# A new start and a split last tile for a one-core transformer block: c loaded as four rows, warm matmuls without a gap, modulation columns ahead of the transposes

## The chip, the cores and the metric

The kernel runs on one core of a Trainium2 chip. The time is the device time of one execution in microseconds. A profile of one execution is taken besides; its span is some 1.7 us shorter than the time of the same execution. TensorE is called PE below, VectorE DVE, ScalarE ACT, GpSimd POOL and SyncE SP.

## The reference

One block with conditioned layer norms, on 2048 tokens of width 512. Cut to what matters:

```python
mod = (_silu(c) @ w_mod).reshape(1, 6, 1, -1)        # c: (1, 512), w_mod: (512, 3072)
sa, ca, ga, sb, cb, gb = (mod[:, i] for i in range(6))
h = _layernorm(x) * (1 + ca) + sa
x = x + ga * A(h)        # 32 query heads on 8 cached k/v heads, the last 512 keys, then wo
h = _layernorm(x) * (1 + cb) + sb
x = x + gb * (relu(h @ w1) @ w2)                      # 512 -> 1792 -> 512
```

Before the first head can start, the kernel needs x's first four tiles, silu(c), the columns sa and ca (two slices of w_mod times silu(c)), and the transposed, modulated h.

## The kernel before

Instructions are recorded into one stream per engine, each with its waits. In the traces PE took its stream in order: in the changed kernel three tiles of xn were done by 8.95 us, and their transposes began at 10.50, behind the columns that stand ahead of them. The start (cuts marked):

```python
    dma(c_col[:, :], c[0].rearrange("(c p) -> p c", p=P), "c", writes=[R_c], eng=ACT)
    for t in range(TPB):
        dma(x_sb[:, t, :], xv[:, t, :], f"xa{t}", writes=[R_x[t]], eng=ACT if t % 2 else SP)
    load_wm(1); load_wm(0); load_wq(0, 2); load_k(0); load_v(0); load_wq(2, 2)
    ...
    warm(48)                                   # matmuls on the identity that nobody reads
    ln_stat(0); ln_stat(1); silu(); ln_stat(2)
    ln_rstd(0, 0, 3); ln_stat(3); ln_rstd(0, 3, 4)
    for tl in range(3):
        ln_norm(tl)
        ln_tposes(tl, [0, 2])                  # four PE transposes
    for f in mod_cols_mm(0, QBK):              # 32 matmuls of one column
        f()
    ln_norm(3)
    ln_tposes(3, [0, 2])
    mod_cols_evac(0, QBK)
    ln_mod_ps([0, 2], hT[0], R_hT[0], 1)
    ...
    q_mms(0); q_mms(1, 5)
```

The main loop has 128 steps, one head of one block of 512 tokens each. Its tasks are put at steps. After each eight heads the output projection of these heads runs beside the next steps; it reads oT, which a DMA transpose on SP's queue has made from o. Two tasks, the loads of the MLP weights, SP issues between those transposes:

```python
    def load_w2():
        for i in range(2):
            f0, f1 = i * FC // 2, (i + 1) * FC // 2
            dma(w2_sb[:, f0:f1, :], w2v[:, f0:f1, :], f"w2{i}", writes=R_w2[f0:f1] + R_wm)
    ...
    add(60, load_w1)
    add(64, load_w2)
```

Both halves name R_wm as written, so SP waits for the first half to land before it issues the second.

## Time and profile before

| | before |
|---|---|
| time, median of 3 | 571.43 us (570.85 to 571.64) |
| traced execution | 569.93 us, span 568.2 |
| first scores (first matmul of q and k) | 16.26 us |
| PE's last matmul to the end of the span | 3.66 us |
| instruction fetches (the queue marked "instruction", number 8) | 34 packets, 0.56 MB |

### The profile page before, as it was taken

How to read it: one execution, taken by the hardware profiler on the slowest of the kernel's cores; microseconds unless marked ns; L12 is line 12 of the kernel's file. 1: busy time of each engine (PE TensorE's matmuls, PEld its weight loads, DVE VectorE, ACT ScalarE, POOL GpSimd, SP SyncE). 2: the span in 40 equal slices, each digit the busy share in tenths (PEclk: the TensorE clock that was granted, in tenths of full speed). 3: DMA queues.
4: the chain of work that ended last, by engine and by line, in shares of the span. 5: the costliest groups of instructions: out<-in, count | busy, mean ns of one | idle time of the engine just before them, and what ended most of it. 6: DMA issues, size and time to landing. Idle time of an engine off the chain costs nothing.

```text
span 568.2 us, 9662 instructions
## 1 busy us (share of the span) xinstructions
PE 553.0 (97%) x4094; PEld 318.7 (56%) x4169; DVE 242.9 (43%) x532; ACT 347.3 (61%) x445; POOL 38.7 (7%) x41
## 2 busy tenths in 40 slices
PE   6999999999999999989999999999999999999997
PEld 5565555666655555546666555555555654444443
DVE  4344465533334655323336553333354438322133
ACT  2876666666666666656666666666666654432500
POOL 1000000002300000023000000330000000000000
PEclk8999999999999999999999999999999999999999
DMA  8795768331231145742321432121114220210001
GB/s 227 202 192 119 179 131 171 81 74 38 39 76 38 38 81 124 167 108 42 75 39 37 75 75 39 38 38 38 38 37 67 47 39 1 38 38 22 22 28 47
DMA packets 111620, 42.67 MB, mean 75 GB/s; under 512 B 94032, under 2 KB 111184, under 8 KB 111568
## 3 DMA queue, kind: packets, MB, share of 16 engines
q1 hardware_dynamic: 110752, 41.70, 34.4%
q8 instruction: 34, 0.56, 0.4%
q10 hardware_dynamic: 816, 0.26, 0.2%
q14 instruction: 18, 0.15, 0.1%
HBM read 18.35 MB, written 2.10 MB: 36 GB/s over the span
## 4 chain that ended last, share of the span: by engine, by line
PE 96%; DMA 2%; DVE 1%; issue 1%; ACTq 0%
PE psS L1350 28%; PE psO L1350 26%; PE psQ L1350 23%; PE psW L1350 19%; DMA oT<-o 1%; DMA x<-in_A_x_dram 1%; DVE st L1360 0%; PE psS L1353 0%; DVE hT L1397 0%; DVE PT L1631 0%; DVE PT L1632 0%; DVE mv L1361 0%; DVE o L1475 0%; ACTq L1296 0%; DVE xn L1371 0%
## 5 line engine op out<-in xcount | busy, mean ns | idle before, releaser
L1464 ACT ACTIVATE PT<-psS 128x1024 bf16<-128x1024 f32 x256 | 262.8, 1028 | 131.7 <-PE psS L1350 131.7
L1350 PE MATMUL psS<-qT,kT 128*128 128x512 bf16 x509 | 151.2, 379 | 0.2
L1350 PEld LDWEIGHTS psO<-v,PT 128*128 128x128 bf16 x2048 | 126.6, 98 | 30.2
L1350 PE MATMUL psO<-v,PT 128*128 128x129 bf16 x2048 | 137.0, 220 | 0.0
L1350 PE MATMUL psQ<-hT,wq 128*128 128x512 bf16 x507 | 130.8, 381 | 1.1 <-DVE hT L1397 1.1
L1474 DVE RECIPROCAL rinv<-psO 128x4 f32<-128x4 f32 x128 | 23.3, 182 | 234.5 <-PE psO L1350 234.5
L1350 PE MATMUL psW<-wo,oT 128*128 128x512 bf16 x451 | 118.1, 379 | 5.3 <-DMA oT<-o 2.1
L1475 DVE TENSOR_TENSOR o<-psO,rinv 128x512 bf16<-128x512 f32 x128 | 88.5, 691 | 4.7 <-DVE rinv L1474 0.3
L1350 PEld LDWEIGHTS psQ<-hT,wq 128*128 128x128 bf16 x508 | 49.7, 98 | 61.1 <-issue 1.0
L1350 PEld LDWEIGHTS psS<-qT,kT 128*128 128x128 bf16 x512 | 49.7, 98 | 59.5 <-ACT PT L1464 0.7
L1456 ACT ACTIVATE qT<-psQ 128x512 bf16<-128x512 f32 x127 | 75.4, 593 | 1.2 <-PE psQ L1350 1.2
L1350 PEld LDWEIGHTS psW<-wo,oT 128*128 128x128 bf16 x512 | 44.9, 98 | 35.4 <-DMA oT<-o 2.6
L1620 ACT ACTIVATE wq<-psS 128x512 bf16<-128x512 f32 x56 | 33.4, 597 | 49.2 <-PE psS L1350 49.2
L1497 DVE TENSOR_TENSOR acc<-psW,acc 128x512 f32<-128x512 f32 x48 | 33.1, 690 | 9.0 <-PE psW L1350 9.0
L1350 PE MATMUL psO<-wmw,wq 128*128 128x512 bf16 x136 | 31.0, 379 | 0.3
L1366 POOL TENSOR_TENSOR rstd<-rstd,cst 128x4 f32<-128x4 f32 (+2 forms) x9 | 8.6, 961 | 273.5 <-DVE rstd L1365 273.4
L1500 POOL TENSOR_TENSOR acc<-acc,gaf 128x512 f32<-128x512 f32 x12 | 15.2, 1268 | 171.0 <-DVE acc L1497 171.0
L1350 PE MATMUL psS<-h2T,wmw 128*128 128x512 bf16 x110 | 25.2, 379 | 0.1
L1350 PE MATMUL psS<-hT,wmw 128*128 128x512 bf16 x110 | 24.4, 379 | 0.1
L1631 DVE TENSOR_TENSOR PT<-psO,gbf 128x512 f32<-128x512 f32 x10 | 6.9, 691 | 40.2 <-PE psO L1350 40.2
L1360 DVE BATCH_NORM_STATS2 st<-x 128x6 f32<-128x512 bf16 x32 | 21.7, 680 | 4.6 <-DMA x<-in_A_x_dram 4.6
L1350 PEld LDWEIGHTS psO<-wmw,wq 128*128 128x128 bf16 x140 | 13.7, 98 | 16.5
(60 smaller groups left out, 168.8 us busy)
## 6 DMA issues: line engine op xcount, KB each, us to landing
wo<-in_A_wo_dram SPq DMA_DIRECT2D x4, 1024.0 KB, 5.9
wq<-in_A_wq_dram SPq DMA_DIRECT2D x7, 512.0 KB, 5.8
wmw<-in_B_w_dram SPq DMA_DIRECT2D x4, 896.0 KB, 5.2
wmw<-in_w_mod_dram SPq DMA_DIRECT2D x6, 512.0 KB, 5.2
oT<-o SPq DMA_TRANSPOSE x128, 2.4
out_dram<-PT SPq DMA_DIRECT2D x16, 128.0 KB, 1.7
x<-in_A_x_dram SPq DMA_DIRECT2D x3, 512.0 KB, 4.2
v<-in_A_v_cache_dram SPq DMA_DIRECT2D x8, 128.0 KB, 4.6
```

The lines of the kernel that those rows point to most:

```text
L1350: kb.op(PE, lambda e: e.matmul(out_ap, lhsT, rhs, start=start, stop=stop), reads=reads, group_writes=[R_b[k] for k in bk], signal=signal)
L1360: kb.op(DVE, lambda e: e.bn_stats(st[:, t, :], x_sb[:, t, :]), reads=[R_x[t]], writes=[R_st[t]])
L1366: kb.op(POOL, lambda e: e.tensor_tensor(rstd[:, sl], rstd[:, sl], cst[:, 0:1].to_broadcast([P, hi - lo]), op=ALU.pow), reads=R_rstd[sl] + ...
L1456: kb.op(ACT, lambda e: e.activation(qT[u % NQT][:, :], bank[bk], ACTF.Copy), reads=[R_b[bk]], writes=[R_qT[u % NQT]])
L1464: kb.op(ACT, lambda e: e.activation(PT[u % NPT][:, pr * 2:pr * 2 + 2, :], s_ps[pr][:, :, :], ACTF.Exp, scale=scale), reads=[R_b[pr * 2], R ...
L1474: kb.op(DVE, lambda e: e.reciprocal(rinv[:, u, :], o_ps[:, :, P]), reads=[R_b[5], R_b[6]], writes=[R_rinv])
L1475: kb.op(DVE, lambda e: e.tensor_tensor(o_sb[u % NOS][:, :, :], o_ps[:, :, 0:P], rinv[:, u, :].unsqueeze(2).to_broadcast([P, TPB, P]), op=A ...
L1497: kb.op(DVE, lambda e: e.tensor_tensor(acc[:, tl, :], bank[WBK], acc[:, tl, :], op=ALU.add), reads=[R_b[WBK], R_acc[tl]], writes=[R_acc[tl]])
L1500: kb.op(eng, lambda e: e.tensor_tensor(acc[:, tl, :], acc[:, tl, :], gaf[:, :], op=ALU.mult), reads=[R_acc[tl], R_ga], writes=[R_acc[tl]])
L1620: kb.op(ACT, lambda e: e.activation(h1T[b % 2][:, fc, :], bank[bk], ACTF.Relu), reads=[R_b[bk]], writes=[R_h1[b % 2][fc]], pre=all_events( ...
L1631: kb.op(DVE, lambda e: e.tensor_tensor(yt[i], bank[bk], gbf[:, :], op=ALU.mult), reads=[R_b[bk], R_gb], writes=[R_yt[i]], pre=pt_done if c ...
```

## The change

The intent: to load c as four rows instead of 512 single elements, so that the loads behind it come sooner (queue 10, which carries c and two tiles of x, has 816 packets before the change); to keep PE busy from the first warm matmul to the first real one, so that it does not lose its clock (before the change PE is idle from 6.43 to 9.41 us, and its clock is half from 9.41 to 16.23); and to shorten what follows PE's last matmul. The diff, cut to its core:

```diff
-    kb.op(ACT, ... activation(tmp, c_col, Exp, scale=-1.0), reads=[R_c], ...)
+    cT = bank[bk].bitcast(BF)[:, 0:DC]
+    kb.op(PE, ... transpose(cT, c_row[:, :], ident[0:DC, 0:DC]), reads=[R_c, R_ident], group_writes=[R_b[bk]])
+    kb.op(ACT, ... activation(tmp, cT, Exp, scale=-1.0), reads=[R_b[bk]], ...)
 ...
-    dma(c_col[:, :], c[0].rearrange("(c p) -> p c", p=P), "c", writes=[R_c], eng=ACT)
+    dma(c_row[:, :], c[0].rearrange("(c p) -> c p", p=P), "c", writes=[R_c], eng=ACT)
 ...
-    warm(48)
+    warm(16)
     ln_stat(0)
+    silu(5)
+    warm(44)
     ln_stat(1)
-    silu()
 ...
+    for f in mod_cols_mm(0, QBK):
+        f()
+    warm(8)
     for tl in range(3):
         ln_norm(tl)
         ln_tposes(tl, [0, 2])
-    for f in mod_cols_mm(0, QBK):
-        f()
+        warm(4)
+    mod_cols_evac(0, QBK)
     ln_norm(3)
     ln_tposes(3, [0, 2])
-    mod_cols_evac(0, QBK)
 ...
-    def y_group(b, tl):
+    def y_group(b, tl, c0=0, c1=D):            # and [:, c0:c1] on all that it touches
 ...
+    mlp.pop()
+    mlp.extend(lambda c0=c0: y_group(NB - 1, TPB - 1, c0, c0 + D // 2) for c0 in (0, D // 2))
 ...
-    pop_mlp(4)
+    pop_mlp(8)
```

More of the change, by code (lines that the diff above doesn't have):

```diff
@@ L1254, in build_fast @@
     ones = T("ones", [P, P])
-    c_col = T("c_col", [P, DC])
+    c_row = T("c_row", [DC, P])
     sc_bf = T("sc_bf", [P, DC])
@@ L1404, in build_fast, with silu @@
     QA = 2
-    def silu():
-        kb.op(ACT, lambda e: e.activation(tmp[:, :], c_col[:, :], ACTF.Exp, scale=-1.0), reads=[R_c], writes=[R_tmp])
+    def silu(bk):
+        cT = bank[bk].bitcast(BF)[:, 0:DC]
+        kb.op(PE, lambda e: e.transpose(cT, c_row[:, :], ident[0:DC, 0:DC]), reads=[R_c, R_ident], group_writes=[R_b[bk]])
+        kb.op(ACT, lambda e: e.activation(tmp[:, :], cT, ACTF.Exp, scale=-1.0), reads=[R_b[bk]], writes=[R_tmp])
         kb.op(DVE, lambda e: e.tensor_scalar(tmp[:, :], tmp[:, :], 1.0, None, op0=ALU.add), reads=[R_tmp], writes=[R_tmp])
         kb.op(DVE, lambda e: e.reciprocal(tmp[:, :], tmp[:, :]), reads=[R_tmp], writes=[R_tmp])
-        kb.op(DVE, lambda e: e.tensor_tensor(sc_bf[:, :], c_col[:, :], tmp[:, :], op=ALU.mult), reads=[R_tmp, R_c], writes=[R_sc])
+        kb.op(DVE, lambda e: e.tensor_tensor(sc_bf[:, :], cT, tmp[:, :], op=ALU.mult), reads=[R_tmp, R_b[bk]], writes=[R_sc])
     def mod_cols_mm(which, bk):
@@ L1629, in y_group @@
         for fc in range(FC):
-            mm(bank[bk], h1T[b % 2][:, fc, tl * P:(tl + 1) * P], w2_sb[:, fc, :], fc == 0, fc == FC - 1, [R_h1[b % 2][fc], R_w2[fc]], [bk], fc == FC - 1)
-        kb.op(DVE, lambda e: e.tensor_tensor(yt[i], bank[bk], gbf[:, :], op=ALU.mult), reads=[R_b[bk], R_gb], writes=[R_yt[i]], pre=pt_done if cnt["y"] <= NY else ())
-        kb.op(DVE, lambda e: e.tensor_tensor(yo[i], yt[i], x_sb[:, t, :], op=ALU.add), reads=[R_yt[i], R_x[t]], writes=[R_yo[i]])
-        dma(ov[:, t, :], yo[i], f"y{i}", reads=[R_yo[i]])
+            mm(bank[bk][:, c0:c1], h1T[b % 2][:, fc, tl * P:(tl + 1) * P], w2_sb[:, fc, c0:c1], fc == 0, fc == FC - 1, [R_h1[b % 2][fc], R_w2[fc]], [bk], fc == FC - 1)
+        kb.op(DVE, lambda e: e.tensor_tensor(yt[i][:, c0:c1], bank[bk][:, c0:c1], gbf[:, c0:c1], op=ALU.mult), reads=[R_b[bk], R_gb], writes=[R_yt[i]],
+              pre=pt_done if cnt["y"] <= NY else ())
+        kb.op(DVE, lambda e: e.tensor_tensor(yo[i][:, c0:c1], yt[i][:, c0:c1], x_sb[:, t, c0:c1], op=ALU.add), reads=[R_yt[i], R_x[t]], writes=[R_yo[i]])
+        dma(ov[:, t, c0:c1], yo[i][:, c0:c1], f"y{i}", reads=[R_yo[i]])
     cut = {}
```

## The prediction

> **What bounds the kernel now.** I read the page first, then the list of waits of PE, then the chain of waits, the timeline of the first 18 us and of the last 14, and last the windows, for the clock. The page's first rows:
>
> ```profile
> span 568.2 us, 9662 instructions
> PE 553.0 (97%) x4094; PEld 318.7 (56%) x4169; DVE 242.9 (43%) x532; ACT 347.3 (61%) x445; POOL 38.7 (7%) x41
> PEclk8999999999999999999999999999999999999999
> ...
> PE 96%; DMA 2%; DVE 1%; issue 1%; ACTq 0%
> ```
>
> PE is busy for 97% and its clock is short in the first slice alone. From 16.3 us to 564.6 us the chain is PE itself. Nothing in the change makes that stretch shorter, so 548 of the 568 us cannot move by much. What can move is the start and the last 4 us. PE's waits (engine, line, released by: us, times, longest):
>
> ```profile
> PE psS L1353 <- DVE xn L1371: 3.0, 1, 3.0
> PE psW L1350 <- DMA oT<-o: 2.1, 1, 2.1
> PE psW L1350 <- POOL cst L1542: 1.4, 1, 1.4
> PE psQ L1350 <- DVE hT L1397: 1.1, 1, 1.1
> ```
>
> The 2.1 is at 244.5 us, behind the large loads of the second MLP weight, and the change does not touch it. The other three lie in the first 13.3 us. The windows there (the column after POOL is the granted clock, then DMA share and GB/s):
>
> ```profile
> 2.50:4.00 1.50, 1.50 (x17) 1.50 (x15) 0.69 (x1) 1.30 (x2) 0.00 (x0) 1.00 0.35 67
> 5.50:8.50 3.00, 0.93 (x12) 0.76 (x9) 2.78 (x9) 0.00 (x0) 0.47 (x1) 1.00 1.09 368
> 12.85:16.25 3.40, 2.97 (x7) 1.24 (x9) 0.69 (x2) 1.39 (x3) 0.00 (x0) 0.50 1.15 321
> 16.25:19.75 3.50, 3.50 (x17) 1.31 (x16) 0.00 (x0) 3.29 (x5) 0.00 (x0) 1.00 1.14 308
> ```
>
> Two things are to be seen. From 2.5 to 4.0 us the DMA engines moved 67 GB/s, though x and the modulation weights were already issued; later they move 368. And PE ran at half clock from about 9.4 until 16.26, just while the two first Q products were made. The timeline of PE says the same:
>
> ```profile
> 9.41 1.46 PE L1353 MATMUL psS<-ident,xn 128*128 128x128 bf16 x12 [2.98 <-DVE xn L1371]
> 10.67 1.04 PE L1350 MATMUL psQ<-sc_bf,wmw 128*128 128x1 bf16 x32
> 14.56 1.86 PE L1350 MATMUL psO<-hT,wq 128*128 128x512 bf16 x4
> 16.26 0.59 PE L1350 MATMUL psS<-qT,kT 128*128 128x512 bf16 x2
> ```
>
> Four Q matmuls take 1.7 us (14.56 to 16.26), 0.43 each; in the chain later four take 0.86, 0.215 each. The 48 warm matmuls took 5.02 us, 105 ns each, so they were almost all at the low clock; then PE sat idle 6.43 to 9.41 and lost what they had earned.
>
> [...] half clock from 9.43 to 16.26, which is 6.83 us, two windows[...]. [...] here the window 9.43 to 12.85, most of it transposes and one-column matmuls, did not raise the clock[...]. c as a column is 512 elements of 2 bytes; queue 10 (ACT's) has 816 packets, which is 512 for c and some 300 for its two tiles of x. The trace agrees: the slow 2.5 to 4.0 us are those of c, which landed 3.6 us after its issue at 0.79.
>
> **The change, part by part.**
>
> *c as four rows.* It takes away 508 descriptors, and adds one transpose on PE and two reads from PSUM (some 0.2 us, beside other work). c should land near 3.0 us (x's first tile, 128 times larger, landed 2.5 us after an issue at the same time). The stretch 2.5 to 4.0 at full rate brings everything behind it forward by 1.5 x (1 - 67/368) = 1.2 us. x's second tile, whose landing at 5.53 held DVE, was queued behind c; I put it at 4.0. The second modulation weight took 7.1 us from 2.17, landing at 9.3; I put it at 8.1.
>
> *DVE's chain to xn.* Statistics of tile 0 end at 4.22. silu now comes before tile 1 and takes 0.5 (three ops, 6.38 to 6.92 before), so tile 1 starts at 4.75, not 5.55. From there to the first normalisation took 3.38 (5.55 to 8.93), of which silu was 0.46; now 2.9. The first xn is done at 7.65 + 0.43 = 8.1 instead of 9.36, the fourth near 9.9.
>
> *PE's order.* 16 warm matmuls end at 1.41 + 16 x 0.105 = 3.1, then c's transpose, then 44 more. In the traced run the clock rose at 6.02 (one window before 9.43); with the same phase 26 of the 44 run at 105 ns and 18 at 56, so they end at 7.1; in the worst phase at 8.0. Then the 32 modulation matmuls must wait for the weight: 8.1, plus 0.85 (their 0.83 in the chain) = 8.95. Then 8 warm (0.45), then three times four transposes and four warm, 0.22 each at full clock: 1.35; the last four transposes 0.22: 10.97. Before, they ended at 12.15. So hT starts at 11.0 instead of 12.2. The 20 warm matmuls after the columns cost 1.1 us of this path; that is the price of the clock.
>
> *The Q products.* Before: hT starts at 12.2, the first scores at 16.26, so 4.06 us. After: ACT's second hT is done 1.45 after the start (12.20 to 13.65), 12.45; the last matmul of Q0 ends at 12.7; Q1's four take 0.86 and the first scores start at 13.6. That is 2.6 us, 1.46 less. Gain at the start: 1.2 + 1.46, about 2.65 us. Its loads should follow: kT landed at 10.8 and v at 11.4 before, both needed after 13.6.
>
> *The last tile in halves.* The end before:
>
> ```profile
> 561.35 3.19 PE L1350 MATMUL psQ<-wmw,wq 128*128 128x512 bf16 x14
> ...
> 564.58 0.69 DVE L1631 TENSOR_TENSOR PT<-psQ,gbf 128x512 f32<-128x512 f32 x1 [1.60 <-PE psQ L1350]
> 565.30 0.69 DVE L1632 TENSOR_TENSOR PT<-PT,x 128x512 bf16<-128x512 f32 x1
> ```
>
> After PE's end come two DVE ops and a transfer of 1.7 us. In halves PE does 28 matmuls of 256 columns in the same 3.0 us (weight loads of 98 ns hide under some 107, half of 215). The first half's DVE work and its DMA lie beside PE. For the second, a small DVE op costs 0.16 and 512 columns 0.69, so 256 cost an estimated 0.425; two of them instead of two of 0.69 save 0.53. The transfer is mostly latency and stays. The second half reuses the output buffer of the tile before last, whose transfer (issue near 563.0, 1.7) lands at 564.7, before the add at 565.0. Gain: about 0.55 us.
>
> *More MLP groups ahead of the last output projection (8 for 4).* PE shows no wait there now; the block's h2T was ready at 492, its first reader came at 503.9, so 3.5 us later harms nothing. Worth 0.
>
> Sum: 2.65 + 0.55 = 3.2 us.
>
> **The rivals.** *A new wait takes the place.* The columns now stand ahead of the transposes and PE works in order; if c was not what held the DMA, the weight still lands at 9.3, hT starts at 12.2 as before, and only the clock (1.46) and the end (0.55) are gained: 569.4. For it: the weight, not c, was the last of that group. Against it: 67 GB/s during c. *The clock is lost again* in the waits for the weight and for hT[...]: then Q pays 1.7 more and the transposes 0.9, 569.5 to 570.5. *The loads become the bound*: DMA is full until 19.7 us, and a start 2.65 earlier could meet wq or k late; each was 3 us or more ahead of its use, so I give this little. *The half tile waits for its output buffer*: the margin is 0.3 us; it would cost a few tenths at most.
>
> **Range and chances.** The traced execution took 569.93, the timed ones 570.85 to 571.64. [...] so I add 0.4 to the gain: 571.4 - 3.6 = 567.8 us. Range 566.3 to 569.8: below, the weight lands a us sooner[...]; above, one of the first two rivals. 2% is 11.4 us, more than the whole start is worth: faster 0.01, same 0.98, slower 0.01.
>
> **What would show it right or wrong.** In the changed trace: c's landing near 3 us instead of 4.4, the DMA rate from 2.5 to 4.0 above 250 GB/s, the column matmuls starting near 8.1 and released by the weight, granted clock 1.00 from 9.4 to 16.3, the first scores near 13.6, the middle unchanged with its one wait of 2.1 us, and the last DVE ops near 0.43 us. It would be wrong if the clock drops before Q, if the weight still lands after 9, or if the wait near 244 us grows with the new phase of the loads.

The sum reads: 1.2 + 1.46, about 2.65 us, at the start and 0.55 at the end are 3.2; the 0.4, the estimate of what the phase of the clock costs, makes it 3.6, and 571.4 - 3.6 is 567.8. The 508 descriptors are a count from c's shape; queue 10 had 520 packets fewer in the changed trace (816 and 296). The 56 ns of a warm matmul is what the trace before shows from 6.04 us (starts some 56 ns apart, 105 until then), and later bridge (four in 0.22 us).

A window of the clock, or a half-clock window, is below a stretch of 3.41 us, and its phase is where it lies in a run. That much is in the traces: the clock changes a whole number of 3.41 us apart, in the kernel before at 5.99, 9.41 and 16.23 us (1 and 2 windows), in the changed one at 5.85, 9.26, 12.67, 248.19 and 251.61 (1, 1, 69 and 1). The first change in each shows only in the time of a matmul, 105 ns until then and 56 after. The half clock began at 9.41 in the kernel before, at 9.26 and 9.94 in two traces of the changed kernel, and between 10.7 and 10.8 in null. What makes the clock fall or rise at the end of a window the traces do not tell.

## More of the kernel before

SP's own waits (who, for what: us in total, times, longest) say that SP stood still for the MLP weights:

```profile
SPq L1296 <- DMA wmw<-in_B_w_dram: 9.1, 2, 4.5
```

And this is the DMA view from 244.3 to 248.4 us, the stretch in which PE waits for oT. The row of GB/s has 40 slices of 0.1025 us:

```profile
GB/s 380 400 320 320 350 380 390 365 335 320 292 292 275 163 243 282 290 290 185 158 287 287 287 287 53 8 0 0 0 0 0 0 0 0 0 0 0 0 0 0
...
q1 hardware_dynamic: 1988, 0.74, 74.7%
```

The second half of w2 ends, then the oT transposes pass at some 290 GB/s, and at 246.8 all is done. (A packet's bytes are booked where the packet begins.)

## The result

The changed kernel took 572.25 us (median of 4, 571.35 to 572.91) where the kernel before took 571.49 in the same rounds. The ratio is 1.0014, with a 95% interval of 0.9995 to 1.0034. A second set of rounds (after2, below) gave 570.98 against 570.81, ratio 1.0002. A ratio here is the mean time of one kernel's runs over that of the other's of the same rounds, so it is not quite the ratio of the medians. The kernel is as fast as before; 567.8 was predicted, and 572.25 lies outside 566.3 to 569.8.

The page of the changed kernel:

```profile
PE 560.1 (98%) x4216; PEld 322.2 (56%) x4216; DVE 242.8 (43%) x534; ACT 347.4 (61%) x445; POOL 38.7 (7%) x41
...
PEclk8999999999999999989999999999999999999999
```

PE's busy time grew by 7 us. Part of it is idle time that warm matmuls now fill, but there is another reason: PEclk has an 8 in its eighteenth slice, near 250 us, where the kernel before had a 9. PE's waits:

```profile
PE psW L1350 <- DMA oT<-o: 3.9, 1, 3.9
PE psQ L1350 <- DMA wmw<-in_w_mod_dram: 1.7, 1, 1.7
PE psW L1350 <- POOL cst L1544: 1.4, 1, 1.4
...
PE psQ L1350 <- issue: 0.3, 1, 0.3
```

The wait of 3.0 for xn is gone. A wait of 1.7 for the modulation weight has come, and the one for oT, which the change does not touch, went from 2.1 to 3.9. The windows of the changed kernel (us from:to and length, busy us of PE, PEld, DVE, ACT, POOL, granted clock, DMA share, GB/s):

```profile
2.50:4.00 1.50, 1.50 (x16) 1.29 (x14) 0.29 (x1) 1.28 (x3) 0.00 (x0) 1.00 0.85 259
9.25:12.65 3.40, 3.40 (x51) 3.40 (x49) 0.64 (x3) 0.00 (x0) 0.00 (x0) 0.50 1.17 291
...
248.20:251.60 3.40, 3.27 (x8) 1.19 (x9) 0.69 (x1) 1.08 (x2) 1.77 (x2) 0.50 0.12 22
```

The DMA rate from 2.5 to 4.0 us rose from 67 to 259 GB/s, as it should. But from 9.25 to 12.65 the clock is half, and again for one window of 3.41 us from 248.2, right after the wait for oT. PE started 8 matmuls of 512 columns there. The kernel before started 27 in the 3.4 us after its own wait, 16 of them of 129 columns only, at full clock:

```profile
246.60:250.00 3.40, 3.31 (x27) 2.06 (x29) 0.96 (x3) 2.43 (x3) 2.09 (x2) 1.00 0.08 15
```

PE's timeline of the changed kernel at the start:

```profile
8.86 0.97 PE L1350 MATMUL psQ<-sc_bf,wmw 128*128 128x1 bf16 x32 [1.71 <-DMA wmw<-in_w_mod_dram]
9.69 1.01 PE L1350 MATMUL psW<-ident 128*128 128x128 bf16 x8
10.50 0.63 PE L1353 MATMUL psS<-ident,xn 128*128 128x128 bf16 x4
...
14.00 1.20 PE L1350 MATMUL psQ<-hT,wq 128*128 128x512 bf16 x4 [0.73 <-DVE hT L1397]
15.03 1.03 PE L1350 MATMUL psO<-hT,wq 128*128 128x512 bf16 x4
15.97 0.59 PE L1350 MATMUL psS<-qT,kT 128*128 128x512 bf16 x2
```

Groups of four begin 0.43 us apart (the transposes at 10.50, the warm ones at 10.92), so each matmul takes 106 ns; Q then runs at full clock. The first scores come at 15.97, only 0.3 us sooner than before. The end is as predicted:

```profile
566.57 1.69 PE L1350 MATMUL psO<-wmw,wq 128*128 128x256 bf16 x14
...
568.30 0.42 DVE L1636 TENSOR_TENSOR PT<-psO,gbf 128x256 f32<-128x256 f32 x1 [0.64 <-PE psO L1350]
```

The two DVE ops are 0.42 us each instead of 0.69. PE's last matmul ends at 568.26, so the end takes 2.90 us instead of 3.66.

The two traced executions differ by 3.0 us (568.2 and 571.2; the first is a quick one of its kernel and the second a slow one of its own, the medians differ by 0.8 at most). The account of these 3.0, each from the waits and windows above; what the half-clock window cost is an estimate, half of its 3.41 us:

| term | before | after | difference, us |
|---|---|---|---|
| first scores at | 16.26 | 15.97 | -0.3 |
| wait for oT near 244 us | 2.14 | 3.93 | +1.8 |
| half-clock window from 248.2 | none | 3.41 long | +1.7 |
| wait at 525 us, released by "issue" | none | 0.30 | +0.3 |
| small rest between first scores and PE's end | | | +0.2 |
| PE's end to the end of the span | 3.66 | 2.90 | -0.8 |

The DMA view of the changed kernel in the same stretch as before the change, 244.3 to 248.4 us:

```profile
GB/s 400 380 370 330 340 340 340 370 370 335 320 292 317 263 193 133 108 235 282 440 275 148 20 8 0 0 0 0 3 7 10 10 7 10 10 12 195 290 287 295
...
q1 hardware_dynamic: 1938, 0.78, 135.6%
q8 instruction: 1, 0.02, 1.5%
```

For some 1.4 us (246.6 to 248.0) next to no packet begins, in the midst of the oT transposes. And one packet of the instruction queue falls into this stretch, none before the change. Its record says that it began at 246.29, was of 16,384 bytes and took 0.96 us; 25 of the transposes' packets that began between 246.48 and 246.71 took 1.3 to 1.5 us each instead of the usual 0.02, and all of them ended within 248.01 to 248.06. The packets' own records show one thing more. After the fetch ended, at 247.25, 27 packets went one behind the other, 3 or 4 per 0.1 us, for 0.7 us; then they came at some 113 per 0.1 us again. It looks as if the one engine that had carried the fetch was then working off its share of a transpose while the others waited for it: 0.96 + 0.7 is 1.7 us, about what the wait gained. The records do not name the engine of a packet, so this is a reading. In the kernel before, the fetch that corresponds to it came at 250.1, after the wait.

**The theories.** A: the packets of the instruction queue, 16 KB each, bring PE its own instructions (8,263 matmuls and weight loads were recorded before the change, and there are 34 packets, so some 243 to a packet; the trace before has 228 to 276 from each packet to the next, but for the gaps among the first four and, near and behind the branch at 520 us, the last four). The change gave PE 33 matmuls and 33 weight loads more ahead of the main loop, so every later fetch comes sooner in the program, and one of them now falls into the transposes that PE is waiting for. B: the wait is longer by chance, or because the loop starts earlier. As to the start, theory A': the idle 1.7 us before the columns dropped the clock; B': transposes and one-column matmuls cannot hold the clock in any case.

### The profile page after: what moved, and what is told of

The parts are those of the page before. It is cut to its first block, busy times and chain, and to the rows that moved or that the text cites. A ratio compares the mean times of both kernels' runs of the same rounds, so it can differ in the third digit from the quotient of the medians. Undisturbed runs are those within 1.5% of the kernel's fastest.

```text
span 571.2 us, 9834 instructions
## 1 busy us (share of the span) xinstructions
PE 560.1 (98%) x4216; PEld 322.2 (56%) x4216; DVE 242.8 (43%) x534; ACT 347.4 (61%) x445; POOL 38.7 (7%) x41
## 4 chain that ended last, share of the span: by engine, by line
PE 94%; DMA 4%; DVE 1%; SPq 0%; issue 0%
PE psS L1350 27%; PE psO L1350 25%; PE psQ L1350 22%; PE psW L1350 19%; DMA oT<-o 1%; DMA wmw<-in_w_mod_dram 1%; DMA xnT<-xn 1%; DMA wmw<-in_B_w_dram 1%; SPq L1296 0%; PE psS L1353 0%; DVE o L1477 0%; SPq L1295 0%; DVE hT L1397 0%; DVE hT L1379 0%; DVE PT L1636 0%
## 5 line engine op out<-in xcount | busy, mean ns | idle before, releaser
L1350 PE MATMUL psW<-wo,oT 128*128 128x512 bf16 x512 | 131.0, 380 | 3.9 <-DMA oT<-o 3.9
L1350 PE MATMUL psO<-wmw,wq 128*128 128x512 bf16 (+1 forms) x154 | 32.9, 369 | 0.0
L1350 PEld LDWEIGHTS psO<-wmw,wq 128*128 128x128 bf16 x154 | 15.1, 98 | 16.7
L1636 DVE TENSOR_TENSOR PT<-psO,gbf 128x512 f32<-128x512 f32 (+1 forms) x11 | 7.3, 667 | 39.6 <-PE psO L1350 39.6
```

The costliest lines, as they stand in the source:

```text
L1350: kb.op(PE, lambda e: e.matmul(out_ap, lhsT, rhs, start=start, stop=stop), reads=reads, group_writes=[R_b[k] for k in bk], signal=signal)
L1636: kb.op(DVE, lambda e: e.tensor_tensor(yt[i][:, c0:c1], bank[bk][:, c0:c1], gbf[:, c0:c1], op=ALU.mult), reads=[R_b[bk], R_gb], writes=[R_ ...
```

## The experiments

All are timed in five rounds beside the kernel before; its medians in the four sets of rounds were 570.75, 570.81, 570.73 and 570.87.

| run | median us | ratio to before | first scores | wait for oT | fetch within it |
|---|---|---|---|---|---|
| null | 570.95 | 1.0010 | 15.97 | 2.3 | no |
| tail | 570.48 | 1.0001 | 16.04 | 2.4 | no |
| bridge | 573.59 | 1.0050 | 14.26 | 2.2 | no |
| after2 | 570.98 | 1.0002 | 15.98 | 4.0 | yes |
| afterpad15 | 571.70 | 1.0020 | 14.27 | 4.0 | yes |
| pad33 | 574.24 | 1.0059 | 15.60 | 4.0 | yes |
| less33 | 570.35 | 0.9985 | 17.76 | 2.3 | no |
| w2only | 567.72 | 0.9953 | 16.03 | none | |
| w2late | 565.30 | 0.9909 | 14.30 | none | |
| w2late2 (w2late again) | 565.66 | 0.9914 | 14.50 | none | |
| w2ccol2 | 568.73 | 0.9957 | 18.20 | none | |
| w2warm60 | 565.13 | 0.9901 | 14.24 | none | |
| w2order | 564.43 | 0.9887 | 13.25 | none | |

**null**: the kernel before, unchanged, as a control.

> The kernel before once more, as a control. Theory A (the change made the wait near 244 us longer): its wait for oT stays near 2.1 us and the mean granted clock is 0.994 in all runs (two half-clock windows, both at the start, 9.4 to 16.3 us). Rival B (that wait varies by itself): its runs spread over more than a microsecond, and the wait near 244 us differs from 2.1 by more than 0.5 us. Ratio 1.000 in both.

The wait stayed at 2.3. The ratio of a kernel to itself was 1.0010 (0.9997 to 1.0023), so differences under 0.2% mean nothing here. Two of its five runs had a granted clock of 0.993 and three 0.990, about two or three half-clock windows (one of 3.41 us takes 0.003 off the mean). So the expectation of 0.994 in all runs was wrong. The phase at the start of this kernel varies: its half clock began at 9.41 us in the first trace, between 10.7 and 10.8 in this one. Its runs spread over 1.5 us, but not by the wait for oT, as far as the trace tells.

**tail**: the kernel before with only the last tile in halves.

> The kernel before with the last output tile in two column halves, nothing else. Expected 0.55 to 0.7 us less than the kernel before: from PE's last matmul to the end 2.9 to 3.1 us instead of 3.66. Rival: the second half waits for its output buffer or its transfer is longer, then 0.3 us or less.

In the trace the end took 2.90 us instead of 3.66 (PE's end at 565.86, span 568.75). In the time it can't be seen: 1.0001 (0.9988 to 1.0014), where 0.76 us would be 0.9987. The mechanism is there; the timing is inconclusive.

**bridge**: 74 warm matmuls for 44.

```diff
-    warm(44)
+    warm(74)
```

> The changed kernel with 74 instead of 44 warm matmuls, so that PE is busy until the second modulation weight lands (8.7 us). Theory A (the idle 1.7 us before the modulation columns dropped the clock at 9.3 us): clock 1.00 until the first scores, transposes of four in about 0.22 us, hT from about 11.8, first scores near 14.4 instead of 15.97, 1.5 us less in time. Rival B ([...]the clock drops in any case): a half-clock window stays at the start, first scores at 15.5 to 16, time within 0.4 us of the changed kernel.

At the start A' held: columns at 8.58 after a wait of 0.4, transposes of four every 0.22 us, granted clock 1.00, first scores at 14.26. So in this trace the clock held through transposes mixed with warm matmuls. But the time was 573.59, a ratio of 1.0050 where the changed kernel had 1.0014 and 1.0002. Four of the six runs show a granted clock of 0.997 (573.4 to 574.3 us), the traced one and one other 1.000 (571.9 and 571.5), so most of them lost one window somewhere that the trace does not show. PE's timeline near 520 us shows what I had not expected:

```profile
521.62 0.60 PE L1350 MATMUL psQ<-wmw,wq 128*128 128x512 bf16 x2
525.14 2.10 PE L1350 MATMUL psQ<-wmw,wq 128*128 128x512 bf16 x9 [2.92 <-issue]
```

There the program branches (a flag chooses between this path and a general one). PE starts two matmuls behind the branch and then stands still for 2.9 us; fetches of 16 KB are on record at 519.07 and 522.33. That the 60 instructions more put a fetch in PE's way here is my reading, and no run was made to vary only this. The wait for oT was 2.2: here the fetch came at 238.7, ahead of it.

**w2late**: the changed kernel with the load of w2 four steps later.

```diff
-    add(64, load_w2)
+    add(68, load_w2)
```

> The changed kernel with the load of the second MLP weight at step 68 instead of 64, three steps after an output projection has begun instead of one before it. Theory A (the wait of PE near 244 us comes from oT transposes that stand behind these loads in SP's queue): the wait of 3.9 us and the half-clock window after it (1.7 us) vanish; PE has no wait over 0.5 us between 20 and 450 us; 570.0 or a little under (2 to 3.5 us less than the changed kernel's median). Rival B (the wait is a stall of the DMA engines, whatever stands in the queue): a wait of 2 to 4 us appears near the new place of the loads, time unchanged.

565.30, 0.9909 (0.9896 to 0.9922): a gain of 0.9%, clear of the noise and more than expected, since here the clock also held at the start. All that is left of PE's waits:

```profile
PE psW L1350 <- POOL cst L1544: 1.4, 1, 1.4
PE psQ L1350 <- ACT hT L1400: 0.9, 1, 0.9
PE psQ L1350 <- DVE xn L1371: 0.7, 1, 0.7
```

The wait for oT is gone, so it came from where the loads stand in SP's queue (SP still waits 9.0 us for these loads, but at a time when nobody needs the next oT).

**w2only**: the same edit in the kernel before.

> The kernel before with the load of the second MLP weight at step 68 instead of 64, nothing else. Theory: its wait of 2.1 us vanishes and nothing else moves, so 2.0 to 2.4 us less than the kernel before, about 568.4; then the changed kernel with the same edit (565.3) is 3.1 better than this, which is what the start and the end of the change are worth when the wait is out of the way (predicted 3.2). Rival (the late load itself brings more, or the change's own parts are worth little): 566.5 or less.

567.72, 0.9953 (0.9940 to 0.9967). The wait is gone, first scores at 16.03. This was 0.7 better than the 568.4 that I expected, which lies within the interval. Between this and w2late lies the worth of the change's own start and end where the clock holds: 0.9953 - 0.9909 = 0.44%, or 2.5 us, uncertain by about 1 us since each ratio is uncertain by 0.13% (3.2 were predicted).

**pad33**: the kernel before with 33 matmuls of one column in PE's idle time; only the count of instructions changes.

```diff
     warm(48)
+    for i in range(33):
+        mm(bank[WBK][:, :1], ident[:, :], ident[:, :1], True, True, [R_ident], [WBK], i == 32)
```

> The kernel before with 33 matmuls of one column (and their weight loads) right after its 48 warm matmuls, in time in which PE sits idle; nothing else. It gives PE as many instructions ahead of the main loop as the changed kernel has. Theory A ([...]66 more instructions move the fetch that came at 250.1 us, after the wait for oT, to about 246.3, into the transposes that PE is waiting for): a fetch within 245 to 247.5, the wait near 244 us 3.5 to 4.2 instead of 2.2, in part of the runs a half-clock window after it; 1.5 to 3.5 us more than the kernel before. Rival B (the longer wait comes from the earlier start of the loop, or is chance): the wait stays at 2.1 to 2.5, time equal to the kernel before within 0.4 us.

Theory A held in full: 574.24 us, 3.4 more than the kernel before, with a start that is if anything earlier (15.60). The wait, and the DMA view from 244.3 to 248.4:

```profile
PE psW L1350 <- DMA oT<-o: 4.0, 1, 4.0
```

```profile
q8 instruction: 1, 0.02, 1.5%
```

The fetch began at 246.85, and a half-clock window followed the wait (249.3 to 252.7): 1.7 to 1.9 for the wait (2.1 in the kernel before, 2.3 in null) and an estimated 1.7 for the clock are the 3.4.

**less33**: the changed kernel with 33 warm matmuls fewer, so with as many PE instructions ahead of the main loop as the kernel before.

```diff
-    warm(44)
+    warm(11)
```

> The changed kernel with 11 warm matmuls instead of 44 after the transpose of c: 33 matmuls and 33 weight loads fewer, so that PE has as many instructions ahead of the main loop as in the kernel before. Theory A (place of the instruction fetch): the fetch comes after the wait, near 250 us, the wait near 244 us is 2.0 to 2.6, no half-clock window follows it. The start is worse (PE idle for 4 us, half clock until 13 us or later, first scores at 16 to 18), so the time by itself says little: 570 to 572. Rival B (the earlier loop or another part of the change makes the wait long): the wait is 3.5 or more.

The wait was 2.3, with no half-clock window behind it; the fetch came at 251.8, after the wait had ended at 248.55. The DMA view of 244.3 to 248.4 has one queue again:

```profile
q1 hardware_dynamic: 2046, 1.08, 108.3%
```

Its start is 1.8 us worse than the changed kernel's in the trace, and yet it is no slower (three of its six runs kept the clock at the start, so its untraced starts differ from the traced one). Together with pad33 this settles theory A against B: the count of instructions makes the wait long or short, in either kernel. When the loop starts does not: null and the changed kernel both have their first scores at 15.97 and waits of 2.3 and 3.9, bridge and afterpad15 theirs at 14.26 and 14.27 and waits of 2.2 and 4.0. That the fetch is the means is seen from its place in all nine traces with this wait.

**afterpad15**: 15 one-column matmuls in the changed kernel, to move the fetch out of the wait.

> The changed kernel with 15 matmuls of one column after the 44 warm ones, in the idle time before the weight lands. Theory A (place of the instruction fetch): the fetch comes 30 instructions, some 2 us, earlier, ahead of the transposes; the wait near 244 us falls to 2.0 to 2.6, no half-clock window there; 1.7 to 3.4 us less than the changed kernel. Rival B: the wait stays near 3.9 and the time does not change by more than 0.4 us.

A miss. The wait was still 4.0. The fetch came at 243.9 and the wait had begun at 242.45, so 30 instructions did not move it out. The fetch did come 2.4 us sooner, but the clock held at the start of this trace and the wait too came sooner, by 1.95, so that within the wait the fetch moved by 0.5 only. It does not speak against A (a fetch in the wait, a long wait). Its time spread from 569.33 to 573.09, and the traced run, the quickest, kept the clock through a wait of 4.0 us: the wait fell across two windows, with 1.45 and 1.40 us of PE work in them. In the traces that lost the clock here the window held 0.0 (the changed kernel), 0.7 (after2) and 0.4 us (pad33). So a long wait does not always cost a half-clock window; that the phase decides, by the PE work that is left in the window, is my reading of these four traces.

**after2**: the changed kernel again.

> The changed kernel once more, on the same chip as the runs beside it. Theory A: a fetch near 246 us, a wait of 3.5 to 4.2 us, in most runs a half-clock window at 248; granted clock 0.994 to 0.997. Rival (the first trace was chance): the wait is under 2.6.

Wait 4.0, fetch at 246.1, a half-clock window from 248.9: the first trace was no chance. But four of five runs had a granted clock of 0.997, one half-clock window in all, so the untraced ones lost it only once, at the start or here; which, the clock's mean does not tell. (afterpad15 shows that a wait of 4.0 need not lose it.)

**w2late2**, w2late once more, as the base of the third set (with w2warm60 and w2order).

> The changed kernel with the second MLP weight loaded at step 68, once more, as the base of the three runs beside it. Expected 564.9 to 565.7 and first scores at 14.3 where the clock holds; if the clock holds at the start only by chance of the window's phase, some run shows a granted clock of 0.997 and is 1.7 us longer.

Four of six runs kept the clock (564.85 to 565.68), two did not (granted 0.997, 566.77 and 567.43). So in the changed kernel whether the clock holds at the start differs from run to run; that the phase of the window decides it is my reading.

**w2warm60**: w2late with 60 warm matmuls for 44.

> The same as the base with 60 instead of 44 warm matmuls, so that PE is not idle before the weight lands. Theory A: granted clock 1.0 in every run whatever the phase, first scores at 14.3, time equal to the base where that kept its clock (565.0 to 565.7) with no slower run. Rival B (a later place of the instruction fetch costs): a wait over 1 us elsewhere, near the branch at 518 us above all, and 566 or more.

565.13, all five runs within 564.95 to 565.55 with a granted clock of 1.000, and no wait at the branch. The change's warm matmuls were to run without a gap; with 16 more the gap ahead of the columns is 0.6 us in the trace (0.7 in w2late, 1.7 in the changed kernel, 2.1 in w2late2). Against w2late2 the median gains 0.5 us; this run has none at 0.997.

**w2ccol2**: w2late with c as a column again.

> The changed kernel with the late load of the second MLP weight and c loaded as a column again (512 elements, no transpose on PE); the order of PE unchanged. Theory A (c as rows brings the weight forward): the second modulation weight lands near 9.3 instead of 8.6, first scores 0.6 us later (14.9), the longer idle time before the columns drops the clock in part of the runs: 0.6 to 2.3 us more than w2late (565.3 and 565.66). Rival B (the load of c was hidden): within 0.3 us of it.

568.73, 3.1 more than w2late2 by the medians of two sets, 2.5 by the ratios. The second modulation weight landed at 9.12 (8.7 in the changed kernel and in less33); in the trace the clock dropped and stayed at half through Q, with first scores at 18.2, and no run had more than 0.997. The direct delay of the weight (8.5 in w2late, 8.7 in w2late2), 0.4 to 0.6 us, is small; by way of the clock it costs more than the 2.3 that I had allowed for at most.

**w2order**: w2late with the columns behind the transposes of three tiles, as in the kernel before, and the warm matmuls kept.

```diff
-    for f in mod_cols_mm(0, QBK):
-        f()
     warm(8)
     for tl in range(3):
         ln_norm(tl)
         ln_tposes(tl, [0, 2])
         warm(4)
-    mod_cols_evac(0, QBK)
+    for f in mod_cols_mm(0, QBK):
+        f()
     ln_norm(3)
     ln_tposes(3, [0, 2])
+    mod_cols_evac(0, QBK)
```

> The same as the base with the modulation columns behind the transposes of three tiles again, as in the kernel before (warm matmuls kept). Theory A (with the columns ahead PE waits for a weight that lands after xn is ready): transposes from 8.3, columns near 9.4, first scores near 13.4 instead of 14.3, 0.9 us less than the base. Rival B (the columns ahead were needed: transposes do not hold the clock): a half-clock window at the start, first scores at 15 or later, 0.7 us or more above the base.

564.43, 0.9887 (0.9874 to 0.9899), five runs within 0.2 us: the best of all.

```profile
7.79 0.40 PE L1353 MATMUL psS<-ident,xn 128*128 128x128 bf16 x4 [0.54 <-DVE xn L1371]
...
9.14 0.94 PE L1350 MATMUL psQ<-sc_bf,wmw 128*128 128x1 bf16 x32
...
13.25 0.59 PE L1350 MATMUL psS<-qT,kT 128*128 128x512 bf16 x2
```

The transposes fill the time in which the weight is still on its way. PE idles for 0.5 us there instead of 0.7 to 2.1 (the 8 warm matmuls that stood behind the columns now follow the 44 without a break, which is a part of that), the clock was 1.000 in all five runs, and the first scores come 1.0 us or more sooner than in w2late. The columns ahead of the transposes, a part of the change, were a loss: 1.2 us against w2late2, 0.7 against w2warm60, whose clock held too.

## Why the prediction was wrong, point by point

- **Two steps failed, the middle and the clock at the start.** In the traced execution they cost more or less the same: the start gave 0.3 us where 2.65 was predicted, and the middle lost 1.8 for a longer wait and an estimated 1.7 for the clock. The lost clock had been named as a rival that would end at 569.5 to 570.5, most of which the range (to 569.8) left out; the middle had been given no cost at all.
- **The middle.** The prediction says "The 2.1 is at 244.5 us, behind the large loads of the second MLP weight, and the change does not touch it", and expects "the middle unchanged with its one wait of 2.1 us". The runs showed 3.9 to 4.0, and in both traces of the changed kernel a half-clock window behind it, worth an estimated 1.7 us: up to 3.5 us, more than the 2.5 that the start and end are worth where the clock holds. The change touched it through the number of PE's instructions (pad33, less33). The prediction did name this wait as one that might grow, but for another reason, the phase of the loads.
- **c as four rows: right in kind.** The rate from 2.5 to 4.0 us rose to 259 GB/s, where I took full rate (368). c was there by 3.23, when PE transposed it (3.0 predicted). x's second tile landed at 4.3 (4.0 predicted), the second weight at 8.7 (8.1). The first normalisation began at 7.88 (7.65).
- **The clock at the start: wrong in both traces of the changed kernel.** I let the clock stand at full through a wait of one microsecond; it dropped at 9.26 (9.94 in after2), after a wait of 1.7 (1.3). The length of the wait alone does not decide it: w2late2 kept its clock through a wait of 2.1. That phase has a part in it is my reading. From the first of the eight warm matmuls to the last transpose it then took 3.6 us (9.69 to 13.27), where 2.0 were predicted. Where it held with the columns ahead (bridge, afterpad15, w2late, w2late2, w2warm60) the first scores came at 14.24 to 14.50, where 13.6 was predicted; most of the rest is the weight, which landed at 8.4 to 8.7 and let the columns start at 8.56 to 8.82, not at 8.1. So the second rival, "The clock is lost again", came true in the traces of the changed kernel.
- **Q at full clock: right.** From hT's start to the first scores 2.6 us were predicted; it took 2.67 (13.30 to 15.97).
- **The last tile: right.** 0.42 us per op and 0.76 us of the end, 0.425 and 0.55 predicted. The transfer, which was to stay as it was, took 1.53 us for half a tile instead of 1.71; that is most of the difference. The second half did not wait for its buffer.
- **More MLP groups ahead of the last projection**: worth 0 by the prediction; no run undid this part alone.
- **The phase of the clock**: the runs of the kernel before do differ in the mean of their clock (0.994, or 0.990 to 0.991 in the longer ones as a rule: in null's set 570.75 to 571.55 us against 569.66 to 571.01), but 0.4 us for it, an estimate, could not be seen beside the rest.
- **The chances** were right: within 2%.

What stays open: whether a fetch holds up the transposes as read above. In all four traces with a fetch in the wait its packet took 0.96 or 0.97 us, and then 25 to 27 packets went one by one for 0.7 us, before the rest came on; but no run was made to test this. Open too is which of the two windows the untraced runs of after2 lost.

## What to carry to other kernels

Adding idle-time instructions to an engine is not free: here, with 66 more on PE (pad33), a fetch of 16 KB came at 246.85 us instead of 250.1, among the transposes that PE waits for, and the wait was 4.0 us instead of 2.1. Where a wait hangs on one late transfer, first take that transfer out from behind large loads (here one number in the program, worth 0.5% in the old kernel and about 0.9% in the changed one), and only then polish the start. And where an engine takes its work in order, as PE does here, put the work whose data comes last behind the work whose data is there (w2order: 0.7 to 1.2 us).

## What the traces showed of the hardware

- Instruction fetches: they are packets of 16 KB on a DMA queue of their own (34 in the kernel before, 0.88 to 1.64 us each). One fetch amid DMA transposes came with a longer wait of PE: it was 3.9 to 4.0 us in all four traces with a fetch in the wait, and 2.1 to 2.4 us in all five without.
- The branch near 520 us: a fetch is on record there in every trace (519.68 and 523.23 us in the kernel before); that the branch calls for it was not tested. PE stood idle for 0 to 0.5 us at the branch in most kernels, and in bridge for 2.92 us two matmuls behind it.
- The clock: it fell to half after a window that was half busy, 5.85 to 9.26 in the changed kernel, with 1.7 us of PE work, part of it one-column matmuls. The kernel before kept its clock through a window (244.9 to 248.3) with 1.7 us of dense matmuls, and afterpad15 through two with 1.4 each. What sets them apart the traces do not show.
- Transposes on PE: with four transposes and four plain matmuls by turns the clock came back to full at 12.67 in the changed kernel, after a window of half clock with 3.40 us of PE work, and stayed at 1.00 in bridge.
- DMA transposes beside a fetch: 25 of their packets, of 0.02 us otherwise, took 1.3 to 1.5 us beside one instruction fetch in the changed kernel, and the wait grew by 1.5 to 1.9 us.
